# Batch 4's q turned by the DMA crossbar instead of TensorE, with new orders for every queue: linear attention and channel mix on one core

## Chip, cores and metric

The kernel runs on one core of a Trainium2 chip. The metric is the device time of one execution in microseconds. Before the change the median of three runs is 194.63 us (194.57 to 195.22).

## What is computed

For 8 batches of 8 heads, 576 positions and 64 dimensions, linear attention is followed by a gated channel mix over 512 channels:

```
q_s = softmax(q, over d);  k_s = softmax(k, over the sequence)
x   = q_s @ (k_s^T @ v)                     per head, joined to [8, 576, 512]
xk  = mu_k * x + (1 - mu_k) * x_prev        x_prev: x one position earlier
xr  = mu_r * x + (1 - mu_r) * x_prev
out = sigmoid(xr @ w_r) * (relu(xk @ w_k)^2 @ w_v)
```

w_k is 512 x 1024, w_v 1024 x 512, w_r 512 x 512. Inputs and output are float32; the products are made in bf16.

## The kernel before

The work is cut two ways. The **attention** part goes by batch b (0 to 7) and group g (0 or 1, four heads each). For each (b, g), GpSimd's queue (POOL) loads q, k and v as `load{b}{g}{q,k,v}` of 576 KB (288 KB halves for batch 1) into one of eleven `raw` buffers. ACT takes exponentials (`expq`, `expk`, L337) and casts v to bf16 (`cast`, L343). DVE sums, inverts and scales q (`rsum` L352, `rrec` L356, `scale` L361). The scaled q lies with positions on the partitions; to be multiplied with the 64 x 64 matrix of a head it has to be turned so that channels lie there. That is done in one of two ways:

- On TensorE: 36 transposes (L376) into a PSUM pair `att`, and a copy by ACT (`qt`, L384).
- Over the DMA crossbar: one DMA transpose on SP's queue, SBUF to SBUF (`qt`, L525). `CROSSBAR` lists the (b, g) that go this way: batches 5 to 7 before the change.

TensorE gathers a group's attention work in **blocks** that nothing interrupts. `TKV{b}{g}` and `B{b}{g}` make the transposes and k^T v (`kv`, L406) of a group; B makes first the x of the group before (`x`, L545). For crossed batches, `M{b}` (function `together`) makes k^T v of both groups of batch b and then the x of whatever groups are pending; M8 only x. Before the change that is TKV20, B21, TKV30, B31, B40, B41, M5 (one x), M6 and M7 (two x each), M8. `X11` and `X21` stand alone. What follows a block on DVE is `rz` and `w` (the reciprocal of k's sums and the head matrices; one operation each where the block lies in an `att` pair, two half ones where it lies in two `mm` banks), then on ACT copies of x (`xb`, `xs`), and on DVE `edge`, `diff`, `sc` and `mix` (L566 to L580), which write xk and xr into rings of four batches: `mix{b}{g}0` for xk, `mix{b}{g}1` for xr, with another digit for the halves of group 1 of batch 1.

The **channel mix** goes by units 0 to 9: 512 positions each, 256 in units 4 and 9. `k{unit}{f}` (L673) is one of eight blocks of xk @ w_k, four matmuls; `relu` (ACT, L660) and `sq` (DVE, L664) follow it. `r{unit}{m}` (L709) is 128 positions of xr @ w_r, with `th` (tanh on ACT, L714) behind it. `v{unit}{m}{h}` (L729) is a part of the second product; `o` (DVE, L735) gates it, and `st` stores it in two halves (L745), nearly all from SP's queue. The k, r and v matmuls use four PSUM banks `mm`; a bank is free again when relu, th or o has read it. The first units are cut finer: a k of units 0 and 1 comes in parts (`k11`, `k11.2`, `k11.3`), because the channels of group 1 come later.

The order on each engine and in each queue is a list written out by hand, `ORDER`: one token for each operation, with the buffer it takes behind a colon. An engine works strictly in this order and waits at each operation for what it needs; POOL and SP, which issue DMAs, do too. At most eight loads of POOL are in flight: each also waits for the landing of the one eight before it. A token `a^b` makes a wait additionally for b; none is used before the change, though the function `ordered` reads it. Fills at the start keep TensorE busy while the first loads land.

Of the kernel before, what the change touches and what calls it, by code (L numbers as in the profile page):

```python
# [55 lines left out]
expk010:1 fill.19:3 fill.20:1 fill.21:1 T01:3 kvn00:0 wp000:0 edge00 KV010:2 X000:1.0 x0001  # L56
expk011 KV011 Z01 load10v0 wk11 qt01:1 rz01:1 edge01 kvn01:1 x0000 load11q0:7 load10k0 mu:2
k02:3 cast101:0 expq100:2 k01:0 wp010:1 X010:1.0 k00:1 mucopy wp011 x0101 x0100 fill.22:2 k03:2
expq101 load11q1 wr rsum100:2 wp001 load11k1:8 rrec100 k03.2 relu03:0 sq03:0 k00.2 k02.2
relu00:1 X011:0.1 relu02:2 x0110 rsum101 expk101:2 k01.2 load11k0 cast100 sq02 scale100:2  # L60
load11v0:9 relu01:0 X001:0.3 k06:1 x0010 load11v1 wv0 expq110:0 wv1 x0111 k04:0 x0011 expk100
sq01 wv2 rrec101 scale101 TKV10:1 rsum110:3 rz10:2 w10:0 relu06:2 sq00 expq111 sq06 k05:2
relu04:0 k07:3 qt10:2 relu07:1 relu05:2 r00:1 r01:0 r03:3 rsum111 rrec110 rrec111 expk111:0
expk110 r02:2 sq05 wv3 scale111:0 cast110:1 sq07 scale110 cast111 B11:0.1 rz11:0 w11:1
load20v0:10 load20q0:0 load30q0:2 th01:0 load20k0:1 th02:1 v010:0 sq04 v000:2 th00:2 v030:1
xb10:0 v001 v031 xs10 v011 edge10 diff10:0 sc1000:0 sc1001 load21q0:3 qt11:3 th03:3 X11:1.0
xs11:1 xb111 v032 v002 load21k0:5 xb110 load21v0:4 v033 v020:3 v012 sc1010:1 mix100 edge11
cast200:2 v003 v013 v021 sc1011 diff110:1 diff111 load60k0:6 load30v0:7 v022 o03 k13:1 sc1100:2
o00 st00.2 sc1101 mix1100 mix1101 v023 load30k0:8 o01 load40k0:9 k11:2 st03.2 k11.2 k11.3
sc1110:0 expq200:1 load31q0:10 expq300:2 o02 mix101 k13.2 sc1111 relu11:2 k15:0 sq11:1 rsum200:0  # L70
k13.3 load40q0:0 k10:3 mix111 k10.2 expk200:1 k10.3 k17:2 relu15:1 k12:0 rrec200 k12.2 relu13:0
sq15 expq210:0 k12.3 r12:1 relu10:2 load31k0:2 relu17:1 expk210:2 scale200:1 k16:3 st00
load31v0:1 sq13 rsum210:1 TKV20:0 load51k0:3 sq17 rz20:1 relu12:0 cast210:0 rrec210 relu16:1
w20:2 r13:2 qt20:1 r11:0 st02.2 st02 scale210:2 k14:3 sq10 th11:4 relu14:2 sq12 th12:5 rsum300:2
B21:1.0 r20:0 xs20:0 rz21:2 xb20 load51v0:5 w21:0 qt21:0 rrec300 sq14 edge20 sq16 diff20:0 r10:3
v100:1 scale300:0 th13:6 st01.2 th20:2 X21:0.1 xs21:1 xb21 sc2010:2 v120:2 expk300:0 th10:1
sc2000:1 edge21 sc2001 diff21:1 v130:0 cast300:1 sc2100:0 expq310:1 v131 v101 load40v0:4 sc2101
mix200 expq400:0 expk310:1 o13 mix210 v110:3 v121 o10 sc2011 load70q0:8 load41v0:7 k24:0
load51q0:10 TKV30:1 rsum310:3 rrec310 relu24:0 v111 rz30:0 st13.2 k23:1 load41k0:0 cast310:2
expk400:2 sq24:0 o11 w30:1 sc2111:1 load41q0:2 k27:0 sc2110 o12 relu23:2 k20:3 k26:2 qt30:2  # L80
cast400:0 relu27:1 k21:1 scale310:1 mix211 B31:0.1 st13 sq23 relu21:0 mix201 sq27 k22:0 rz31:1
sq21 relu20:2 xb30:1 relu22:1 st03 w31:2 st11.2 st11 r23:1 xs30 rsum400:0 sq20 rrec400 sq22
th23:6 qt31:3 scale400:2 r22:3 edge30 th22:3 relu26:0 r30:0 diff30:0 sq26 sc3011:0 sc3010 k25:1
B40:1.0 v220:3 relu25:2 xb31:0 xs31 v200:2 th30:4 sc3001:1 v230:1 sq25 load61k0:1 load50q0:9
sc3000 edge31 expk410:0 v231 cast510:1 mix300 diff31:1 sc3100:2 sc3101 rz40:2 v201 cast410:2
expq410:2 load61v0:4 o23 v221 st01 w40:0 mix310 k41:0 r21:1 st12 o20 o22 st22.2 relu41:1
expq510:1 k40:2 v210:0 rsum410:1 rrec410 k42:3 load71q0:0 th21:0 sq41:1 st23 load50v0:5 relu40:0
relu42:2 k46:1 sq40 relu46:1 sc3111:1 qt40:1 st22 k37:2 expq500:0 scale410:0 st20.2 k33:3 k44:1
v211 rsum510:2 sq46 relu37:0 sq42 sc3110 expk510:1 B41:0.1 mix301 sq37:0 k34:2 relu44:1
load50k0:7 rrec510 rz41:0 o21 load60q0:2 relu33:2 mix311 w41:1 k45:1 k43:3 expk500:2 sq33 sq44  # L90
rsum500:3 relu43:0 xs40:1 relu45:2 k30:0 sq45 sq43 relu34:1 xb40 st20 k47:3 rrec500 relu47:2
scale500:1 st10 edge40 r33:1 th33:3 sq47 r31:2 diff40:0 st12.2 scale510:2 st10.2 k31:3 th31:2
relu30:0 load71k0:10 cast500:0 st23.2 r41:1 v410:2 k35:0 v411 sc4011:2 load60v0:9 expq600:2
load71v0:3 load61q0:7 relu31:2 th41:5 rsum600:0 o41 r40:3 sq31 sc4010 qt41:0 th40:1 load70k0:5
k36:1 sq30 relu35:2 mix401 sc4000:0 rrec600 qt50:2 sq34 relu36:0 M5:1.1 st41.2 k32:0 cast600:2
relu32:1 r32:1 st41 rz51:1 rz50:2 sc4001 sq35 xb41:0 w50:2 w51:0 sq32 v400:0 xs41 mix400
# [24 lines left out]
relu80:1 sq80 r82:3 st61.2 th81:5 relu82:1 th82:0 th83:1 sq82 v810:0 v800:1 v811 o81 v820:3 v821
o82 st82 st81 v801 st81.2 o80 r90:2 sq90 v830:0 v831 sq93 th90:6 st80.2 st82.2 st73.2 v900:3
v901 r91:1 o83 o90 st80 st83 st83.2 st90 st73 v910.2:2 th91:2 v911.2 o91.2 st90.2 st91.4 v910:0
v911 o91 st91.3 st91 st91.2
# [786 lines left out]
```

## Time and profile before

| what | value |
|---|---|
| median of three runs | 194.63 us |
| the profiled execution | 195.4 us |
| its span, first to last instruction | 193.6 us |
| granted TensorE clock | 0.995 |
| DMA, mean over the span | 216 GB/s, 41.86 MB |

The page gives busy times by engine, the chain of work that ended last, and the costliest groups of instructions. The chain in order of time, the timeline of an engine (start and length of each instruction, with the idle time before it and what ended that), the busy times by stretches and the DMA issues with their times to landing are views of the same trace. A row of the timeline with xN stands for N instructions merged, by start of the first; a matmul's length includes its way through the array, so the distance from start to start is what it costs.

### The profile page before, as it was taken

The numbers are of one execution on the slowest core, as the hardware profiler recorded it, in microseconds if no ns is written. First come the engines' busy times: TensorE is split into PE (matmuls) and PEld (weight loads), VectorE is DVE, ScalarE is ACT, GpSimd is POOL, SyncE is SP. The second block draws the span as 40 slices with busy tenths as digits, with TensorE's granted clock in tenths as the row PEclk, the third lists the DMA queues.
The fourth block names the chain that finished last, engine by engine and source line by source line (L and its number), as shares of the span: only waits on it lengthen the run. The fifth ranks groups of instructions, "written<-read, shape, count | busy, mean of one in ns | idle before, by whom it ended". The sixth has DMA issues, their size and how long they took to land.

```text
span 193.6 us, 4674 instructions
## 1 busy us (share of the span) xinstructions
PE 184.6 (95%) x1830; PEld 89.6 (46%) x1830; DVE 154.6 (80%) x368; ACT 138.8 (72%) x226; POOL 41.3 (21%) x65
## 2 busy tenths in 40 slices
PE   7698889999999999999999999999999999999991
PEld 2263344444545544655454544454444445554450
DVE  1788965999999999999999899997986494661521
ACT  3688899899999999899999878258425742357010
POOL 8346457453415402421200000000000000000000
PEclk9999999999999999999999999999999999999997
DMA  5999999999999997999990294253065003720085
GB/s 187 311 314 283 298 329 247 404 390 416 398 393 390 406 412 268 317 359 413 284 290 3 50 201 83 62 123 78 0 136 116 3 0 81 166 51 5 11 204 164
DMA packets 23614, 41.86 MB, mean 216 GB/s; under 512 B 9372, under 2 KB 12712, under 8 KB 23592
## 3 DMA queue, kind: packets, MB, share of 16 engines
q0 software_dynamic: 9392, 27.99, 43.3%
q1 hardware_dynamic: 13384, 12.14, 24.6%
q10 hardware_dynamic: 816, 1.44, 2.5%
q8 instruction: 14, 0.23, 0.5%
q14 instruction: 8, 0.07, 0.1%
HBM read 33.56 MB, written 9.44 MB: 222 GB/s over the span
## 4 chain that ended last, share of the span: by engine, by line
PE 84%; DMA 11%; POOL 2%; issue 0%; DVE 0%; POOLq 0%
PE mm_a L729 9%; PE mm_a L673 9%; PE mm_b L673 9%; PE mm_d L729 8%; PE mm_c L729 8%; PE mm_b L729 7%; DMA wk_ab<-in_moe_w_k_dram 6%; PE mm_c L673 6%; PE mm_b L709 6%; PE mm_d L673 5%; DMA wr<-in_moe_w_r_dram 5%; PE mm_d L709 4%; PE mm_a L709 4%; PE mm_c L709 3%; PE att_b L545 1%; PE att_a L545 1%
## 5 line engine op out<-in xcount | busy, mean ns | idle before, releaser
L729 PEld LDWEIGHTS <-k_a 128*128 128x128 bf16 x152 | 14.6, 98 | 15.6 <-issue 0.5
L729 PEld LDWEIGHTS <-k_b 128*128 128x128 bf16 x144 | 13.9, 98 | 16.4 <-issue 0.2
L709 PEld LDWEIGHTS <-xr 128*128 128x128 bf16 x144 | 13.7, 98 | 16.6 <-DMA wr<-in_moe_w_r_dram 0.6
L709 PE MATMUL mm_b<-wr,xr 128*128 128x512 bf16 x48 | 12.5, 379 | 0.1
L673 PEld LDWEIGHTS <-wk_aa 128*128 128x128 bf16 x80 | 7.5, 98 | 8.7 <-issue 1.3
L673 PEld LDWEIGHTS <-wk_bb 128*128 128x128 bf16 x80 | 7.8, 98 | 7.7 <-DMA wk_bb<-in_moe_w_k_dram 0.2
L673 PEld LDWEIGHTS <-wk_ab 128*128 128x128 bf16 x80 | 7.7, 98 | 7.7 <-DMA wk_ab<-in_moe_w_k_dram 0.2
L673 PEld LDWEIGHTS <-wk_ba 128*128 128x128 bf16 x80 | 7.5, 98 | 8.2 <-issue 1.1
L709 PE MATMUL mm_d<-wr,xr 128*128 128x512 bf16 x36 | 9.2, 379 | 0.0
L664 DVE TENSOR_TENSOR k_b<-rel_b 128x512 bf16<-128x512 bf16 (+1 forms) x15 | 5.7, 381 | 4.4 <-ACT rel_b L660 4.2
L709 PE MATMUL mm_a<-wr,xr 128*128 128x512 bf16 x32 | 8.2, 379 | 0.0
L660 ACT ACTIVATE rel_a<-mm_b 128x512 bf16<-128x512 f32 (+1 forms) x8 | 4.7, 583 | 4.4 <-PE mm_b L673 2.3
L664 DVE TENSOR_TENSOR k_a<-rel_c 128x512 bf16<-128x512 bf16 (+1 forms) x14 | 5.6, 399 | 2.4 <-ACT rel_c L660 2.3
L660 ACT ACTIVATE rel_c<-mm_b 128x512 bf16<-128x512 f32 (+1 forms) x9 | 5.3, 590 | 3.0 <-PE mm_b L673 3.0
L673 PE MATMUL mm_b<-xk,wk_ab 128*128 128x512 bf16 x24 | 7.3, 379 | 0.0
L660 ACT ACTIVATE rel_b<-mm_a 128x512 bf16<-128x512 f32 (+1 forms) x7 | 4.2, 602 | 4.2 <-PE mm_a L673 4.2
L709 PE MATMUL mm_c<-wr,xr 128*128 128x512 bf16 x28 | 7.2, 379 | 0.0
L673 PE MATMUL mm_b<-xk,wk_aa 128*128 128x512 bf16 x24 | 7.2, 380 | 0.0
L664 DVE TENSOR_TENSOR k_a<-rel_a 128x512 bf16<-128x512 bf16 (+1 forms) x16 | 6.1, 384 | 1.2 <-ACT rel_a L660 1.2
L673 PE MATMUL mm_a<-xk,wk_ba 128*128 128x512 bf16 (+1 forms) x24 | 6.9, 370 | 0.0
L673 PE MATMUL mm_a<-xk,wk_bb 128*128 128x512 bf16 (+1 forms) x24 | 6.9, 370 | 0.0
L664 DVE TENSOR_TENSOR k_b<-rel_c 128x512 bf16<-128x512 bf16 (+1 forms) x14 | 5.4, 385 | 1.7 <-ACT rel_c L660 1.3
(395 smaller groups left out, 553.1 us busy)
## 6 DMA issues: line engine op xcount, KB each, us to landing
raw_a<-in_q_dram POOLq DMA_DIRECT2D x3, 576.0 KB, 8.9
raw_c<-in_q_dram POOLq DMA_DIRECT2D x3, 576.0 KB, 9.7
raw_e<-in_v_dram POOLq DMA_DIRECT2D x3, 576.0 KB, 11.6
out_dram<-th_g SPq DMA_DIRECT2D x13, 128.0 KB, 2.4
out_dram<-th_d SPq DMA_DIRECT2D x12, 128.0 KB, 5.0
out_dram<-th_b SPq DMA_DIRECT2D x10, 128.0 KB, 4.2
out_dram<-th_a SPq DMA_DIRECT2D x10, 128.0 KB, 2.3
raw_b<-in_k_dram POOLq DMA_DIRECT2D x2, 576.0 KB, 10.9
```

The lines of the kernel that those rows point to most:

```text
L545: kn.nc.tensor.matmul(kn.half(slot, u)[two[r], to:to + n], lhsT=kn.ws[w.index][two[u], r, :], rhs=x_columns(r, u, at, n), start=True, stop ...
L660: kn.nc.scalar.activation(out=kn.rels[rel.index][:, 0:n], in_=kn.bank(kf)[:, 0:n], func=ACT.Relu, scale=HALF_ROOT)
L664: kn.nc.vector.tensor_tensor(out=kn.k2s[k2.index][:, fc, 0:n], in0=kn.rels[rel.index][:, 0:n], in1=kn.rels[rel.index][:, 0:n], op=ALU.mult)
L673: kn.nc.tensor.matmul(kn.bank(kf)[:, 0:n], lhsT=kn.wk[fc // 4][ct % 2][:, ct // 2, (fc % 4) * 128: (fc % 4) * 128 + 128], rhs=kn.xs[0][:, ...
L709: kn.nc.tensor.matmul(kn.bank(rps), lhsT=kn.xs[1][:, ct, c:c + 128], rhs=kn.wr[:, ct, :], start=(ct == 0), stop=(ct == CT - 1))
L729: kn.nc.tensor.matmul(kn.bank(vps)[:, 0:width], lhsT=kn.k2s[k2.index][:, ft, 128 * m:128 * m + 128], rhs=wv_of(ft)[:, part], start=(ft == ...
```

## The change

`CROSSBAR` begins at batch 4, so batch 4's two q are turned by DMAs on SP, and TensorE's blocks become TKV20, B21, TKV30, B31, M4 (k^T v of both groups of batch 4, and the x of group 1 of batch 3), M5, M6, M7 (two x each) and M8. Three waits are added with `^`: the turn of (4, 0) waits for the load of (6, 0)'s q, the load of (6, 1)'s q waits for the turn of (5, 1), and the turn of (6, 0) waits for the load of (7, 1)'s q. The rest of `ORDER` is new on every engine and queue. Cut to its core, with the stretches that the prediction speaks of:

```diff
-CROSSBAR = tuple((b, g) for b in range(5, B) for g in range(2))
+CROSSBAR = tuple((b, g) for b in range(4, B) for g in range(2))
 ORDER = """
...
-load20v0:10 load20q0:0 load30q0:2 ... load20k0:1 ... load21q0:3 ... load21k0:5 ... load21v0:4 ... load60k0:6
+load21q0:10 ... load20q0:0 ... load20v0:2 load21k0:1 ... load30q0:3 ... load20k0:4 ... load51k0:6 ... load21v0:7
...
-k16:3 ... TKV20:0 ... cast210:0 rrec210 relu16:1 ... r13:2 qt20:1 r11:0 ... k14:3 ... B21:1.0 r20:0
+expk200:2 r10:3 k14:1 relu17:0 st02 cast210:0 TKV20:1 rz20:1 relu15:2 rrec210 relu14:1 r13:0 ... r20:2 r11:1 ... B21:0.1
...
-B40:1.0 ... qt40:1 ... B41:0.1 ... qt41:0 ... qt50:2 ... M5:1.1 ... qt51:3 ... M6:1.0.1 ... qt60:1 ... qt61:0
+M4:0.0 ... qt40^load60q0:0 ... qt41:1 qt50:2 ... st22 ... st22.2 ... qt51:3 ... M5:1.1.0 ... load61q0^qt51:10
+... M6:0.1.0 ... load70v0:3 load71k0:8 load70k0:4 ... load71q0:6 ... qt60^load71q0:0 qt61:1
...
-r91:1 o83 o90 st80 st83 st83.2 st90 st73 v910.2:2 th91:2 v911.2 o91.2 st90.2 st91.4 v910:0 v911 o91 st91.3 st91 st91.2
+r91:2 o81 v910.2:3 st83.2 st81 th91:4 v911.2 o91.2 st90.2 st81.2 v910:1 st91.4 st91.3 v911 o91 st91 st91.2
 """
```

More of the change, by code (lines that the diff above doesn't have):

```diff
@@ L49 @@
 ACT!load00q0:0 zero ident load00q1 ACT!load00k0:1 load01q1:2 ACT!load01q0 rows load00v consts
-warm load00k1 load01v late load01k0:3 load10v1:4 wk00 load10q0:5 expq001:0 expq000 load10q1
-rsum001:0 ACT!load01k1 rsum000 wk01 expq011:1 rrec001 load10k1:6 rrec000 rsum011:1 fill:1
+warm load00k1 load01v late load01k0:3 load10q0:4 wk00 load10q1 expq001:0 expq000 load11q0:5
+rsum001:0 ACT!load01k1 rsum000 wk01 expq011:1 rrec001 load10k0:6 rrec000 rsum011:1 fill:1
 fill.2:2 fill.3:3 fill.4:0 fill.5:1 fill.6:2 fill.7:3 fill.8:0 fill.9:1 fill.10:2 fill.11:3
@@ L55 @@
 fill.26:3 fill.27:1 KV001:0 rrec011 scale010:1 KV000 T00:1 rest Z00 qt00:0 scale011 rz00:0
[L56 to L96, printed above, removed]
@@ L121 @@
[L121 to L124, printed above, removed]
+expk010:1 fill.19:3 fill.20:1 fill.21:1 T01:3 kvn00:0 wp000:0 edge00 wp001 wk11 mu:0 fill.22:1
+load10k1 X000:1.0 mucopy expk011 KV010:2 KV011 Z01 qt01:1 x0001 expq100:2 edge01 rz01:1 kvn01:1
@@ new lines @@
+x0000 X001:0.3 x0010 load10v0:7 load10v1 load11q1 expq101 k03:0 wr wp010:1 X010:1.0 k02:1 x0011
+expq110:0 x0100 wp011 x0101 rsum100:2 k00:2 k01:3 k02.2 rrec100 rsum101 relu02:0 sq02:0 k03.2
+k01.2 rrec101 relu03:1 expk100:2 X011:0.1 scale100:2 x0110 relu01:2 k00.2 rsum110:3 expk101
+relu00:0 k05:1 load11v0:8 k04:0 cast100:0 cast101 rrec110 scale101 k06:3 x0111 k07:2 expq111
+load11k0:9 sq01 sq03 sq00 scale110:0 relu06:2 TKV10:0 r03:3 relu05:1 relu07:0 load11k1 rz10:2
+r02:1 sq06 relu04:2 load11v1 w10:0 rsum111 sq05 wv0 qt10:2 cast110:1 expk110:0 sq07 sq04 expk111
@@ new lines @@
+rrec111 r01:2 wv1 r00:0 wv2 cast111 scale111 th03:0 wv3 th02:1 th00:2 B11:1.0 xs10:0 xb10
+load21q0:10 v020:3 rz11:0 w11:1 edge10 v010:1 load20q0:0 v000:0 v001 qt11:3 diff10:0 v021 v011
+load20v0:2 load21k0:1 v022 X11:0.1 sc1000:0 v023 sc1001 sc1010:1 xs11:1 v012 load30q0:3 xb110
+sc1011 mix100 v013 edge11 xb111 th01:3 expq210:1 v002 load20k0:4 expq200:2 o02 load51k0:6
+diff111:1 load21v0:7 diff110 o01 load31q0:5 k13:3 sc1100:2 v003 sc1101 v030:2 o00 load31v0:9
+mix1100 mix1101 k11:1 sc1110:0 v031 v032 v033 k11.2 k11.3 load40q0:8 o03 k10:0 cast200:2
@@ new lines @@
+rsum200:0 sc1111 relu11:1 load40v0:10 st00 expk210:1 rrec200 k13.2 sq11:1 k13.3 k10.2 mix111
+k10.3 relu10:0 k16:2 relu16:2 sq16 k12:1 k12.2 load40k0:0 mix101 sq10 expq300:0 relu13:1 k17:0
+k12.3 load30v0:2 st00.2 load30k0:1 scale200:1 k15:2 load41v0:3 rsum210:1 relu12:2 sq12 sq13
+expk200:2 r10:3 k14:1 relu17:0 st02 cast210:0 TKV20:1 rz20:1 relu15:2 rrec210 relu14:1 r13:0
+w20:2 st01.2 load50v0:4 load31k0:7 st02.2 r20:2 r11:1 scale210:2 qt20:0 th13:4 th20:5 rsum300:2
+B21:0.1 rrec300 sq14 th11:6 rz21:2 th10:2 sq15 w21:0 xb20:1 v110:0 r12:2 scale300:0 v130:1 xs20
@@ new lines @@
+sq17 edge20 v131 qt21:1 X21:1.0 diff20:0 th12:1 sc2001:2 expq400:2 xs21:0 xb21 load50k0:8 sc2000
+v111 o13 mix200 st01 expq310:1 cast400:1 edge21 diff21:1 load41q0:5 v100:3 cast300:2 sc2100:0
+cast310:0 sc2101 load51q0:10 load41k0:2 mix210 sc2011:1 expk300:0 o11 v101 v120:2 v121 o12
+rsum310:3 k25:1 sc2111:2 k24:0 st13 rrec310 k21:2 o10 load61v0:9 relu24:1 sc2010 TKV30:0
+relu21:2 sc2110 st10 st10.2 st11.2 k20:0 st12 sq24:0 k22:3 mix211 k23:2 relu25:0 rz30:0 w30:1
+sq21 k26:1 expk400:2 expk310:1 relu22:1 k27:3 mix201 sq25 relu20:2 sq22 qt30:2 relu27:0
@@ new lines @@
+scale310:1 sq20 r21:0 rsum400:0 sq27 relu26:1 load70q0:1 relu23:2 sq23 r23:3 cast410:2 B31:1.0
+rrec400 th23:3 v230:1 rz31:1 sq26 xs30:0 st03 st03.2 v231 xb30 v200:2 v201 scale400:2 w31:2
+edge30 expk410:0 r30:3 th21:2 diff30:0 qt31:3 load51v0:0 load60v0:7 st12.2 sc3010:0 o23 M4:0.0
+load50q0:3 o20 sc3001:2 r22:2 load60k0:2 expq410:0 th30:0 load71v0:5 xs31:1 xb31 th22:1
+cast510:0 sc3000 st11 cast500:1 v220:3 v221 mix300 rz40:2 rz41:0 w40:0 w41:1 load61k0:0 st20.2
+v210:0 edge31 diff31:1 sc3101:1 expq510:1 sc3100 load60q0:4 v211 mix310 sc3110:2 k47:1 relu47:0
@@ new lines @@
+k44:2 o22 k40:3 sc3111 relu44:2 o21 k45:1 sq44:1 k41:2 rsum410:1 sq47 st13.2 rrec410 k42:0
+relu40:1 st21 sc3011 expq500:2 k30:3 relu45:2 k31:1 sq40 mix311 st21.2 sq45 relu42:0 sq42
+relu30:1 sq30:0 k34:0 relu31:2 mix301 sq31 k43:3 relu43:0 relu41:1 rsum500:2 k35:1 k46:3 r41:2
+relu35:2 th41:6 sq43 rrec500 r31:1 sq41 relu46:0 k33:2 th31:4 k32:3 scale410:0 relu34:1 st20
+r33:1 expk500:1 k37:0 sq46 scale500:1 qt40^load60q0:0 relu32:0 rsum510:3 v410:3 v411 sq34
+expq600:0 qt41:1 qt50:2 sq35 st22 relu37:1 k36:0 rrec510 th33:2 r40:1 scale510:2 sq37 o41 st22.2
@@ new lines @@
+rsum600:0 expk510:0 qt51:3 relu33:2 M5:1.1.0 sq32 load61q0^qt51:10 cast610:2 sq33 rz50:1 w50:2
+rz51:2 relu36:1 th40:5 xb40:1 sq36 rrec600 xs40 edge40 diff40:1 xs41:0 w51:0 sc4001:1 v300:0
+v400:1 v401 xb41 expq700:2 cast600:0 v301 sc4011:2 o40 edge41 v310:2 expk610:2 o30 st40.2 sc4000
+diff41:0 v311 r32:3 sc4101:0 mix400 v330:1 sc4100 v320:0 sc4010 th32:1 sc4110:1 sc4111 mix410
+expk600:0 v321 st40 v331 o32 o31 expq610:1 k55:3 k50:0 o33 st41.2 st30.2 relu55:0 relu50:2 k57:2
+relu57:1 M6:0.1.0 k52:3 mix411 sq55:1 mix401 xb51:0 load70v0:3 load71k0:8 load70k0:4 rsum610:1
@@ new lines @@
+st31.2 rz61:0 rz60:1 w61:1 relu52:0 k53:2 k51:3 w60:0 st31 xs51 st41 xs50:1 r51:0 scale600:0
+sq52 sq50 r52:1 xb50 relu51:0 relu53:2 st33.2 edge50 diff50:1 edge51 sq51 th51:5 diff51:0 st32
+sq57 cast710:1 sc5001:0 sc5101:1 sq53 r53:3 k54:2 th53:4 th52:6 st33 expk710:1 k56:0 rrec610
+sc5000 sc5010:2 r50:3 sc5100 mix510 relu54:0 mix500 v520:1 load71q0:6 relu56:1 v500:2 sc5011
+sq54 sc5111:1 k64:0 sq56 v501 scale610:1 expq710:0 th50:2 k61:3 mix501 o50 relu64:2 cast700:0
+relu61:0 rsum710:2 k65:0 relu65:1 expk700:0 rrec710 qt60^load71q0:0 qt61:1 st50 v521 v530:2 v531
@@ new lines @@
+k75:1 o61 o60 k73:0 k74:3 relu75:0 relu73:2 th63:0 qt70:3 sq73 relu74:2 sq76 M8:0.1.0 k70:2
+v620:3 xb70:1 st61 xs70 edge70 diff70:1 sc7010:1 mix611 v621 o62 sc7000:2 relu70:1 st61.2 v630:2
+xs71:0 v631 sc7001 o63 xb71 sq70 edge71 k77:0 relu77:1 st63 st62.2 r80:1 r72:3 r73:2 th80:5
+th73:4 r71:0 v700:1 st63.2 sq75 sq74 diff71:0 st62 sc7100:0 th71:0 th72:2 sc7101 mix710 mix700
+k94:2 sc7011 relu94:0 k96:0 k95:3 k92:2 sq77 v701 relu96:2 v730:0 sq96:0 o70 relu92:1 sq92
+v710:2 v731 v711 o73 st73.2 k90:1 relu95:2 v720:3 v721 sc7111:0 st70.2 st60 k86:0 mix701 o71
@@ new lines @@
+k91:2 sq94 sc7110 o72 mix711 k84:3 relu91:1 sq95 sq91 st23 st72 st71.2 relu90:0 st60.2 relu86:2
+k97:2 relu97:1 sq97 relu84:1 k80:1 sq86:1 sq90 relu80:2 sq84 k81:0 relu81:0 k82:2 relu82:1 sq82
+k93:3 relu93:1 sq93 sq80 r81:1 k87:0 k85:2 relu85:1 relu87:2 sq81 sq85 k83:3 relu83:0 st71
+st72.2 st23.2 sq87 r82:2 th81:1 sq83 v820:0 st73 v800:3 r83:1 v821 th83:0 th82:2 v801 v830:1 o80
+st80.2 st70 o82 r90:2 v900:3 v901 th90:3 o90 st82 st90 st80 v831 st82.2 o83 st83 v810:0 v811
+r91:2 o81 v910.2:3 st83.2 st81 th91:4 v911.2 o91.2 st90.2 st81.2 v910:1 st91.4 st91.3 v911 o91
@@ L125 @@
+st91 st91.2
 """
```

30 lines of the change are left out of this document (6 added, 24 removed).

## The prediction

> **What bounds the kernel now.** I read the page first: the span, the busy times, the chain that ended last.
>
> ```profile
> span 193.6 us, 4674 instructions
> PE 184.6 (95%) x1830; PEld 89.6 (46%) x1830; DVE 154.6 (80%) x368; ACT 138.8 (72%) x226; POOL 41.3 (21%) x65
> PE 84%; DMA 11%; POOL 2%; issue 0%; DVE 0%; POOLq 0%
> ```
>
> The chain is TensorE for 84% and DMA for 11%. The chain in order of time tells where the change-over is:
>
> ```profile
> 18.00 9.29 DMA wr<-in_moe_w_r_dram
> 27.33 1.04 PE mm_b L709 x4
> ...
> 189.61 0.42 DVE th_c L735
> ```
>
> Until 27.33 us the load of `wr` decides; from there TensorE runs without a visible gap to 189.57, then one gate, one store and its landing fill the rest of the 193.6. The table by stretches shows how little room the others have early on:
>
> ```profile
> 40.00:55.00 15.00, 14.97 (x200) 6.95 (x198) 14.97 (x30) 14.61 (x23) 5.78 (x8) 1.00 1.04 401
> ```
>
> The columns are PE, weight loads, DVE, ACT, POOL, granted clock (1.00), DMA share, GB/s. Between 40 and 55 us PE, DVE and ACT are all full and the DMA engines move 401 GB/s. So work taken from TensorE after 27.33 is worth its full time, and an operand that comes late there costs its full lateness: nothing makes it good afterwards.
>
> **The change, part by part.**
>
> *Batch 4 leaves TensorE's transposes.* Blocks B40 and B41 (the x of the group before, 36 transposes, 36 kv products each) go; M4 (both kv, one x) comes, and M5 takes two x in place of one. A block is measured here from where the next plain matmul would have started, which is 0.43 us after the start of a row with x2 (0.22 for x1), to the start of the first plain one behind it.
>
> ```profile
> 71.70 0.38 PE L673 MATMUL mm_b<-xk,wk_bb 128*128 128x512 bf16 x1
> ...
> 73.00 0.60 PE L729 MATMUL mm_d<-wv_a,k_a 128*128 128x512 bf16 x2
> ...
> 84.25 0.59 PE L729 MATMUL mm_a<-wv_d,k_a 128*128 128x512 bf16 x2
> ...
> 85.77 0.60 PE L673 MATMUL mm_c<-xk,wk_ba 128*128 128x512 bf16 x2
> ...
> 96.15 0.59 PE L673 MATMUL mm_b<-xk,wk_bb 128*128 128x512 bf16 x2
> 97.77 0.61 PE L673 MATMUL mm_a<-xk,wk_aa 128*128 128x512 bf16 x2
> ```
>
> ```profile
> 109.44 0.59 PE L729 MATMUL mm_b<-wv_d,k_a 128*128 128x512 bf16 x2
> 111.26 0.61 PE L673 MATMUL mm_a<-xk,wk_ba 128*128 128x512 bf16 x2
> ```
>
> ```profile
> 128.17 0.59 PE L729 MATMUL mm_b<-wv_d,k_b 128*128 128x512 bf16 x2
> 129.90 0.61 PE L673 MATMUL mm_b<-xk,wk_aa 128*128 128x512 bf16 x2
> ```
>
> B40: 73.00 - 71.92 = 1.08. B41: 85.77 - 84.68 = 1.09. M5, with one x: 97.77 - 96.58 = 1.19. M6 and M7, with two x: 1.39 and 1.30. Now 1.08 + 1.09 + 1.19 = 3.36; afterwards 1.19 + 1.35 = 2.54. The change takes **0.82 us** from TensorE (0.78 to 0.87).
>
> *What goes with it on the other engines.* ACT loses two copies of q, and DVE does batch 4's weights in halves:
>
> ```profile
> 82.14 1.11 ACT L384 COPY qt_b<-att_b 128x1152 bf16<-128x1152 bf16 x1
> ```
>
> ```profile
> 77.37 0.28 DVE L423 TENSOR_TENSOR w_a<-att_b,rz_c 128x128 bf16<-128x128 f32 x1
> 99.04 0.28 DVE L428 TENSOR_SCALAR w_c<-mm_c,rz_c 128x64 bf16<-128x64 f32 x1
> ```
>
> ACT gains about 2 us; DVE pays two more operations of 0.28 and two small reciprocals, under 0.8 us. Neither is on the chain, so nothing for both; if DVE were late the 0.8 us would count, and it stands in the upper end.
>
> *The front.* Before `wr`, POOL's queue has in both orders the same batch 0 v, eight loads of 288 KB and four of `wk`; only which one stands where differs. So `wr` should land at 27.3 again. The new order does all of unit 0's k before batch 1's first block, and that block waits for v, which moves to two places ahead of `wr`; it still ends before 27.3. Cost: nothing, from -0.2 to +0.3. The tail has the same last five PE operations and the same two last stores on SP: nothing, up to 0.3 if SP's queue backs up.
>
> *The new order of loads, 40 to 52 us.* Here I find a wait. In the new order POOL loads batch 5's k (load51k0) ahead of load21v0, which becomes the eighth load from load21q0 on instead of the seventh from load20v0. On ACT, `cast210` waits for it; behind `cast210` stand relu15, relu14 and qt20; relu15 frees the PSUM bank that r20 takes on PE. First when PE is ready for r20, by pitches:
>
> ```profile
> 30.89 0.22 PE L545 MATMUL att_a<-qt_c,w_a 64*64 64x64 bf16 x4
> ...
> 32.04 0.61 PE L729 MATMUL mm_a<-wv_a,k_a 128*128 128x512 bf16 x2
> ...
> 34.21 0.59 PE L729 MATMUL mm_a<-wv_b,k_a 128*128 128x512 bf16 x2
> ...
> 35.10 0.60 PE L729 MATMUL mm_b<-wv_c,k_a 128*128 128x512 bf16 x2
> ```
>
> ```profile
> 60.01 0.59 PE L673 MATMUL mm_a<-xk,wk_bb 128*128 128x512 bf16 x2
> ...
> 61.32 0.60 PE L729 MATMUL mm_d<-wv_c,k_b 128*128 128x512 bf16 x2
> ```
>
> ```profile
> 51.32 1.04 PE L709 MATMUL mm_a<-wr,xr 128*128 128x512 bf16 x4
> ```
>
> B11 is 1.15 (30.89 to 32.04), X11 0.46 (35.10 - 34.64), a block like TKV20 0.87 (61.32 - 60.44, rounded down), a matmul 0.216. In the new order 72 matmuls stand between B11 and r20: 30.89 + 1.15 + 0.46 + 0.87 + 72 x 0.216 = 48.9. In the old one 76 and B21 (1.08) did, which makes 50.87; the row says 51.32. So the kernel before lost **0.45 us** here to small waits of its own; their operations stand elsewhere in the new order, and I let them go.
>
> Now when ACT is ready. Loads land one after the other; with no stores beside them they come 1.51 us apart, as two that ACT waited for show:
>
> ```profile
> 38.21 1.16 ACT L337 ACTIVATE eq_b<-raw_a 128x1152 bf16<-128x1152 f32 x1 [0.35 <-DMA raw_a<-in_q_dram]
> 39.73 1.16 ACT L337 ACTIVATE eq_c<-raw_c 128x1152 bf16<-128x1152 f32 x1 [0.35 <-DMA raw_c<-in_q_dram]
> ...
> 47.53 1.14 ACT L343 CAST vv_a<-raw_e 128x1152 bf16<-128x1152 f32 x1
> 48.63 0.60 ACT L660 ACTIVATE rel_b<-mm_d 128x512 bf16<-128x512 f32 x1
> ```
>
> The eighth load in the trace of before, its issue on POOL and its time to landing:
>
> ```profile
> 35.76 0.72 POOL L211 DMA_DIRECT2D raw_g<-in_k_dram  x1 [0.61 <-ACT xb_b L557]
> ```
>
> ```profile
> raw_g<-in_k_dram POOLq DMA_DIRECT2D x1, 576.0 KB, 12.6
> ```
>
> It landed at 35.76 + 12.6 = 48.4, though six loads after 38.2 would make 47.2 without stores: the unit 0 stores, issued from 39.09 to 43.45, took the rest.
>
> ```profile
> 39.09 0.54 SPq L745 DMA_DIRECT2D out_dram<-th_c  x1
> ...
> 42.85 0.59 SPq L745 DMA_DIRECT2D out_dram<-th_a  x1
> ```
>
> The new order has as many stores there, starting some 0.9 us later behind a later gate, so load21v0 lands between 47.2 and 48.4; I take 48.1, near the row with stores. Then cast210 from 48.15, relu15 1.10 later (47.53 to 48.63), 0.60 long: the bank is free at 49.85. PE stands from 48.9: **0.93 us** (0.2 to 1.2). Inside it lies a smaller wait ahead: k11's second part needs mix1100, which gets one more gate in front of it on DVE.
>
> ```profile
> 37.51 0.67 DVE L735 SCALAR_TENSOR_TENSOR th_d<-th_d,mm_b 128x512 f32<-128x512 f32 x1
> 38.11 0.35 DVE L575 TENSOR_SCALAR xm_c<-xd_b,mu 128x576 bf16<-128x576 bf16 x1
> ...
> 39.27 0.81 DVE L580 TENSOR_TENSOR xk<-xm_c,xb_b 128x576 bf16<-128x576 bf16 x2
> ```
>
> One gate is 0.60 (37.51 to 38.11), so both halves end near 40.7, where PE wants the second at 40.5: about 0.2, swallowed by r20's wait or left alone if that one goes.
>
> *Turns kept apart.* On SP the turn of 40 waits for load60q0, and 41, 50, two stores and 51 queue behind it; on POOL load61q0 and four loads queue behind the turn of 51. M5 is the first to want 40 and 41. In the trace its plain start is 96.58; the new order has k32 and M4 ahead of it in place of B40 and B41 (0.86 + 1.19 - 2.17 = -0.1) and the wait above (0.93 - 0.45), which makes 97.0. A turn lands 3.2 us after issue:
>
> ```profile
> qt_c<-qs_c SPq DMA_TRANSPOSE x1, 3.2
> ```
>
> ```profile
> 81.60 1.35 DVE L361 TENSOR_TENSOR qs_a<-eq_c,rrec_b 128x1152 bf16<-128x1152 bf16 x1
> ```
>
> The scaled q of 41 ended at 82.95; the new order puts fifteen more DVE operations ahead of it (one reduction like the 1.35 of this row, the others of the 0.3 to 0.8 kind of the rows above), an estimated 6 us, and perhaps 2 us of waits: 89 to 91, landed by 94.2. The 2.8 us left hide the turn, so nothing is charged.
>
> **Sum**: -0.82 - 0.45 + 0.93 = -0.34. The profiled execution's own 195.4 becomes 195.1, its span 193.6 becomes 193.3; the median of the runs, 0.8 below that execution, 194.63, becomes **194.3**.
>
> **Rivals.** (1) *The load is in time.* load21v0 lands at 47.2 and r20 stands for no more than the 0.25 of k11: -0.82 - 0.45 + 0.25 = -1.0, **193.6**. For it: the 1.51 us pitch of loads; against it: 48.4 in the trace with stores in flight. (2) *The turns come late*, and the kernel is slower. Place: M5. Each us by which the turn of 41 is issued after 93.8 costs one us of PE, since M5 heads PE's queue. It takes 2.8 us more delay on DVE, or turns that run one behind the other at more than 3.2 us: with two queued turns of 5 us, landed at 91 + 8 = 99, M5 waits 2.0: 194.3 + 2.0 = **196.3**. For it: the one turn with a landing was alone; against it: 2.8 us of room. [...] (3) *The old waits do not go, and new ones of their kind come*: the 0.45 stays and as much again is lost where DVE and ACT are full: 194.3 + 0.9 = **195.2**. (4) *Nothing gained*: blocks cost what they did; 0.82 more, **195.1**; the block rows speak against it.
>
> **How the numbers follow.** Forecast 0.45 (193.9 to 194.7 by the load's landing); rival 1 0.23, 2 0.12, 3 0.15, 4 0.05. A measurement of this kernel tells about 0.5% from no change: 193.66 and 195.60. Below: most of rival 1, 0.17. Above: rival 2 and a third of rivals 3 and 4, with a little for the DVE charge, 0.22. Between: 0.61. The range leaves out the best tenth and the rest of rival 2: 193.4 to 196.0.
>
> **What would show it.** B40 and B41 gone, M4 about 1.2 us long, M5 about 1.35. `wr` landing at 27.3 and r03 starting then. ACT idle before cast210 with a DMA named, and PE idle ahead of r20 with ACT named, near 49 us, 0.5 to 1 us. No PE idle before M5. The prediction is wrong if PE shows other gaps after 27.33 that add to over half a us, or if the chain holds a crossbar turn.

## The result, and the profile after

The changed kernel takes 195.72 us in the median of 17 runs (194.88 to 196.61), the kernel before 194.87 us beside it (194.38 to 195.28). The ratio is 1.0047, with an interval of 1.0035 to 1.0059: slower by a half per cent, where 194.3 was forecast, slightly faster.

The profiled execution of the changed kernel (194.88) is the fastest of its 17, and that of the kernel before (195.40) is slower than any of the 17 beside it. So a second profile of each, from one chip, stands beside them below. First the page of the changed kernel, with span, busy times and the chain that ended last:

```profile
span 193.1 us, 4559 instructions
PE 183.9 (95%) x1758; PEld 89.1 (46%) x1758; DVE 153.7 (80%) x372; ACT 137.4 (71%) x226; POOL 41.3 (21%) x65
...
PE 76%; DMA 11%; DVE 6%; POOL 2%; ACT 1%; issue 1%; POOLq 0%; ACTq 0%
```

TensorE lost 0.7 us of busy time and ACT 1.4, as the crossbar took its work. The chain holds DVE for 6% now. Its way in order of time, from the load of `wr` on:

```profile
17.79 8.55 DMA wr<-in_moe_w_r_dram
26.39 1.04 PE mm_d L709 x4
...
40.46 1.26 DVE rsum_a L352
44.45 1.27 DVE qs_b L361
45.72 1.26 DVE rsum_b L352
49.04 1.02 PE mm_c L709 x4
...
187.20 0.89 PE mm_b L729 x8
```

`wr` decides the start as before, and the chain leaves TensorE ahead of 49.04, where r20 begins. From 36 to 48 us it runs along DVE. It gets there from `relu15` by a semaphore row of ACT's sequencer at 48.09 that belongs to `qt20`, and passes by the cast that ran on ACT until 48.49. So the 6% of DVE are not what r20 waited for; the rows below and the experiment on the load tell that. The stretch that had no room before, in the busy times from 40 to 55 us:

```profile
40.00:55.00 15.00, 14.24 (x192) 6.84 (x190) 14.12 (x27) 13.97 (x23) 5.17 (x8) 1.00 1.04 401
```

PE is busy for 14.24 us of 15 where it was 14.97. The 0.73 us that are missing can be one hole or several. TensorE's timeline, and then ACT's, show one:

```profile
47.24 1.04 PE L709 MATMUL mm_a<-wr,xr 128*128 128x512 bf16 x4
49.04 1.02 PE L709 MATMUL mm_c<-wr,xr 128*128 128x512 bf16 x4 [0.76 <-ACT rel_c L660]
```

```profile
47.34 1.15 ACT L343 CAST vv_a<-raw_h 128x1152 bf16<-128x1152 f32 x1 [0.86 <-DMA raw_h<-in_v_dram]
48.40 0.59 ACT L660 ACTIVATE rel_c<-mm_c 128x512 bf16<-128x512 f32 x1
```

This is the wait that the prediction placed: `cast210` waits for load21v0, relu15 comes behind it, and r20 on PE behind relu15. From start to start r13 to r20 takes 1.79 (before rounding) where four matmuls take 0.86: 0.93 us. The blocks, on TensorE's timeline:

```profile
74.16 1.03 PE L709 MATMUL mm_d<-wr,xr 128*128 128x512 bf16 x4
...
76.08 1.04 PE L709 MATMUL mm_c<-wr,xr 128*128 128x512 bf16 x4
...
95.12 1.03 PE L709 MATMUL mm_b<-wr,xr 128*128 128x512 bf16 x4
...
97.29 0.60 PE L729 MATMUL mm_a<-wv_a,k_a 128*128 128x512 bf16 x2
```

Measured as in the prediction, M4 takes 76.08 - 75.02 = 1.06 and M5 97.29 - 95.98 = 1.31. No PE idle stands ahead of M5: the turns are in time. Now the end, on SP's queue and on DVE:

```profile
184.84 0.59 SPq L745 DMA_DIRECT2D out_dram<-th_c  x1
185.54 2.38 SPq L745 DMA_DIRECT2D out_dram<-th_a  x2
188.01 1.19 SPq L745 DMA_DIRECT2D out_dram<-th_b  x2
189.30 1.33 SPq L745 DMA_DIRECT2D out_dram<-th_e  x2
```

```profile
188.11 0.42 DVE L735 SCALAR_TENSOR_TENSOR th_e<-th_e,mm_b 128x256 f32<-128x256 f32 x1 [0.40 <-PE mm_b L729]
```

The last gate ends at 188.53, and the last two stores are issued from 189.30 to 190.63. In the kernel before, the gate of 189.61 ended at 190.03, and the second of the last two stores followed it by 0.18 us:

```profile
189.56 1.19 SPq L745 DMA_DIRECT2D out_dram<-th_c  x2
```

After the change SP is over a us behind: two stores at 185.54 took 2.38 us to issue, where two take 1.2 elsewhere. Where the time went, from the four profiles:

| us | before | before, second | after | after, second |
|---|---|---|---|---|
| own time | 195.40 | 194.58 | 194.88 | 195.14 |
| first r starts | 27.33 | 26.77 | 26.39 | 26.98 |
| from there to the end of the last matmul | 162.24 | 161.99 | 161.69 | 161.89 |
| from there to the end of the span | 4.0 | 4.1 | 5.0 | 4.4 |

The start differs by chance more than by kernel. The middle is a little shorter than before. The end is longer by 0.3 to 1.0 us, where nothing had been expected, or 0.3 at most.

### The profile page after: what moved, and what is told of

Its sections match the earlier page's. It is cut to its first block, busy times and chain, and to the rows that moved or that the text cites. A ratio compares the mean times of both kernels' runs of the same rounds, so it can differ in the third digit from the quotient of the medians.

```text
span 193.1 us, 4559 instructions
## 1 busy us (share of the span) xinstructions
PE 183.9 (95%) x1758; PEld 89.1 (46%) x1758; DVE 153.7 (80%) x372; ACT 137.4 (71%) x226; POOL 41.3 (21%) x65
## 4 chain that ended last, share of the span: by engine, by line
PE 76%; DMA 11%; DVE 6%; POOL 2%; ACT 1%; issue 1%; POOLq 0%; ACTq 0%
PE mm_d L729 9%; PE mm_a L729 8%; PE mm_d L673 7%; PE mm_b L729 7%; PE mm_a L673 7%; DMA wk_ab<-in_moe_w_k_dram 6%; PE mm_c L729 6%; PE mm_c L673 6%; PE mm_c L709 6%; PE mm_b L673 5%; PE mm_b L709 4%; DMA wr<-in_moe_w_r_dram 4%; PE mm_d L709 3%; PE mm_a L709 2%; PE att_a L545 1%; PE att_b L545 1%
## 5 line engine op out<-in xcount | busy, mean ns | idle before, releaser
L709 PE MATMUL mm_c<-wr,xr 128*128 128x512 bf16 x48 | 12.3, 379 | 0.8 <-ACT rel_c L660 0.8
L660 ACT ACTIVATE rel_b<-mm_c 128x512 bf16<-128x512 f32 (+1 forms) x9 | 4.6, 507 | 9.8 <-PE mm_c L673 9.4
L709 PE MATMUL mm_b<-wr,xr 128*128 128x512 bf16 x40 | 10.3, 379 | 0.0
L660 ACT ACTIVATE rel_a<-mm_d 128x512 bf16<-128x512 f32 (+1 forms) x10 | 5.6, 555 | 4.0 <-PE mm_d L673 3.8
L673 PE MATMUL mm_a<-xk,wk_bb 128*128 128x512 bf16 (+1 forms) x28 | 8.1, 371 | 0.0
L673 PE MATMUL mm_a<-xk,wk_ba 128*128 128x512 bf16 (+1 forms) x28 | 8.1, 371 | 0.0
L673 PE MATMUL mm_d<-xk,wk_aa 128*128 128x512 bf16 (+1 forms) x28 | 7.7, 356 | 0.0
L673 PE MATMUL mm_d<-xk,wk_ab 128*128 128x512 bf16 (+1 forms) x28 | 7.7, 356 | 0.0
L664 DVE TENSOR_TENSOR k_a<-rel_b 128x512 bf16<-128x512 bf16 (+1 forms) x15 | 5.7, 381 | 1.9 <-ACT rel_b L660 1.7
L553 ACT CAST xb_a<-att_a 128x1024 bf16<-128x1024 f32 x5 | 5.3, 1052 | 2.0 <-DVE xr L580 1.4
```

Source lines behind the costliest of these rows:

```text
L553: kn.nc.scalar.copy(out=kn.xbs[xb.index][:, h, 64:576], in_=kn.whole(pair)[:, h, :])
L660: kn.nc.scalar.activation(out=kn.rels[rel.index][:, 0:n], in_=kn.bank(kf)[:, 0:n], func=ACT.Relu, scale=HALF_ROOT)
L664: kn.nc.vector.tensor_tensor(out=kn.k2s[k2.index][:, fc, 0:n], in0=kn.rels[rel.index][:, 0:n], in1=kn.rels[rel.index][:, 0:n], op=ALU.mult)
L673: kn.nc.tensor.matmul(kn.bank(kf)[:, 0:n], lhsT=kn.wk[fc // 4][ct % 2][:, ct // 2, (fc % 4) * 128: (fc % 4) * 128 + 128], rhs=kn.xs[0][:, ...
L709: kn.nc.tensor.matmul(kn.bank(rps), lhsT=kn.xs[1][:, ct, c:c + 128], rhs=kn.wr[:, ct, :], start=(ct == 0), stop=(ct == CT - 1))
```

## The experiments

The theory at first: the load behind r20 and a backed-up SP queue cost what the blocks give. All are edits of the changed kernel unless it says before. Each was timed beside runs of the kernel before on the same chip.

**The kernels as they are.**

> The changed kernel as it is. Theory A (front): its first profile had wr landing at 26.3 us, 0.9 us earlier than the kernel before, and was the fastest of 17 runs; a typical execution has wr at about 27.2, and that is the 0.85 us by which the median (195.72) stands above that profile (194.88). Theory B (tail): the spread is in the last stores, which SP issues late; then wr lands near 26.3 again and the time from the end of the last matmul to the end of the span moves between 4 and 6 us. Ratio to before by either: 1.003 to 1.006.

> The kernel before as it is, for a second profile: its first (195.4) was slower than its median (194.87) by 0.5. If it is typical this time: about 194.8, wr landing at 27.3 or a little ahead, small waits of PE of 0.3 to 0.8 us after 27 us, 4.05 us from the end of the last matmul to the end of the span.

Measured: the changed kernel 195.32 (194.93 to 195.79), ratio 1.0026 (1.0011 to 1.0040); before 194.58, a typical run. Both theories of the spread are half right: `wr` landed at 26.93 and the first r came 0.6 us later than in the first profile, and the end shrank from 5.0 to 4.4. The wait for r20 grew, on TensorE's timeline of the second profile:

```profile
47.72 1.04 PE L709 MATMUL mm_a<-wr,xr 128*128 128x512 bf16 x3
49.84 1.02 PE L709 MATMUL mm_c<-wr,xr 128*128 128x512 bf16 x4 [1.08 <-ACT rel_c L660]
```

The idle time is 0.32 more than in the first profile, so r20 stands 1.25 us.

**The load behind r20.**

```diff
-load51k0:6 diff111:1 load21v0:7
+diff111:1 load21v0:7 load51k0:6
```

> The changed kernel with load51k0 behind load21v0 on POOL. Theory (the load sets r20's wait): load21v0 lands 1.5 us earlier, near 45.8, PE's 0.93 us ahead of r20 near 49 us goes to 0.1 or less, and the time falls by 0.5 to 0.9 us: about 194.8 to 195.2, ratio to before 0.999 to 1.002. Rival (the next late thing takes its place, as DVE and ACT are full between 40 and 55 us): the wait moves to B21 or a k a few us later, the time falls by under 0.3: 195.4 or more.

Measured: 194.08 (193.34 to 195.06), ratio 0.9959 (0.9941 to 0.9977), 1.24 less than the changed kernel on the same chip, more than expected, since the wait is 1.25 in a typical run and not 0.93. On PE and ACT of this run:

```profile
47.49 1.04 PE L709 MATMUL mm_a<-wr,xr 128*128 128x512 bf16 x3
48.37 1.03 PE L709 MATMUL mm_c<-wr,xr 128*128 128x512 bf16 x4
```

```profile
46.59 1.17 ACT L343 CAST vv_a<-raw_h 128x1152 bf16<-128x1152 f32 x1
47.64 0.63 ACT L660 ACTIVATE rel_c<-mm_c 128x512 bf16<-128x512 f32 x1
```

The cast no longer waits, r20 follows r13 after 0.88, and no other wait takes its place. The middle takes 160.66 us, 1.33 less than the second profile of before.

**Stores issued earlier.**

```diff
-st23 st72 st71.2 ... st60.2 ... st23.2 ... st73 ... st70
+st23 st60.2 st23.2 st70 st73 st72 st71.2
```

> The changed kernel with st60.2, st23.2, st70 and st73 ahead of st72 on SP, so that they are issued at 170 to 173 us, where SP stood waiting, and not between 180 and 185. Theory (SP's queue backs up at the end): four issues of 0.6 us leave the tail, the last store is issued within 0.2 us of its gate, the time from the last matmul to the end of the span falls from 5.0 to about 4.0, and the time falls by 0.7 to 1.1 us: about 194.7 to 195.0. Rival (the end is set by the landing of the last stores, whatever their issue): no change, 195.5 to 195.9.

Measured: 195.45 (194.56 to 196.20), ratio 1.0025 (1.0005 to 1.0045): no change, and still 5.0 us at the end. SP again spent 1.66 us on one store, and the last store was issued 1.5 us behind its gate. The edit did less than was meant: from 180 us on SP issues twelve stores in the changed kernel and eleven here, and the nine from 184 us on are the same, since three of the four moved stores had been issued before 171 us anyhow. So this run decides neither theory. It shows that the stall lies in the issue of a single store, and something slows that issue itself. The table of DMA queues of the second profile of the changed kernel, from 185 to 188 us, shows what else was there (queue, kind, packets, MB, share of 16 engines):

```profile
q1 hardware_dynamic: 255, 0.43, 59.5%
q8 instruction: 1, 0.02, 1.9%
```

One packet of kind "instruction", 16 KB, held a DMA engine for 1.9% of 16 x 3 us = 0.9 us. Such packets come through the whole run, by the packets' records some 6 to 25 us apart. In the kernel before, the last one of this queue lies between 173 and 175 us, with no store under way:

```profile
q8 instruction: 1, 0.02, 4.4%
```

The change takes 144 rows out of TensorE's instruction stream (3660 to 3516 by the two pages, weight loads included). With two rows for each matmul of 0.216 us, TensorE goes through 9.3 per us. That this queue brings TensorE's instructions, in step with its rows, was the author's estimate here; if it does, fewer rows let the same fetch come later. A store can meet it: in the kernel before, one that runs alone keeps DMA engines busy, from 125.1 to 125.5 us, for 101.7% of the time of 16 (a packet counts whole where it starts), so it uses all of them, also one that a fetch holds. That became the new theory to be tested: the cost of a fetch depends on where it falls.

**The fetch moved, first try.** The fills at the start are cut in four, which adds rows and no work.

```diff
-matmul(bank[:, 0:512], ...)
+for a in range(n): matmul(bank[:, 0:512 // n], ...)      # n = 4 for the first 14 fills (22 in the kernel before), else 1
```

> The changed kernel with 14 of the 27 fills at the start (matmuls on zeros that only keep TensorE busy; 512 columns each) cut in four of 128 columns. The same work, but 84 rows more in TensorE's instruction stream. Theory (a fetch of TensorE's instructions, a 16 KB packet of queue 8 of 0.9 to 1.5 us, falls into the last stores at 184 to 186 us and holds up one of the 16 DMA engines that every store uses): TensorE reads 9.3 rows per us, so the last fetch comes 9 us sooner, near 176, where no store is under way; the slow issue on SP (1.5 to 2.4 us for one or two stores) goes, the last store is issued within 0.2 us of its gate, and the time from the last matmul to the end falls from 4.3 to 5.1 to about 4.05. The time falls by 0.3 to 1.0: 194.5 to 195.2, ratio to before 0.998 to 1.002. Rival (the tail is long because of the order of the stores, and the fetch only happens to be there): no change, 195.3 to 195.8.

> The kernel before with 22 of its fills cut in four: 132 rows more in TensorE's stream. Its last fetch was at 174 us, between two groups of stores; 14 us sooner it comes at 160, and one more fetch comes near 182 to 185, into the last stores (from 182 us on). Theory (the fetch): a slow issue on SP appears, 4.05 us from the last matmul to the end become 4.4 to 5.1, and the time rises by 0.3 to 1.0: 195.1 to 195.8, ratio 1.002 to 1.005. Rival (the order of the stores): no change, ratio 0.999 to 1.001.

> The changed kernel with load51k0 behind load21v0 and 14 fills cut in four: both repairs. If the load and the fetch are the two things that cost, the gains add: 194.08 less 0.3 to 1.0, that is 193.1 to 193.8, ratio to before 0.991 to 0.995. If the fetch is nothing: 194.1, ratio 0.996.

Measured: 195.89 (ratio 1.0043, 1.0021 to 1.0065), 198.81 (1.0201, 1.0176 to 1.0226) and 194.55 (1.0005, 0.9972 to 1.0038). The end did what the theory says: 4.0 us in the first and the third, 5.2 in the kernel before. The totals did not, because the edit is not neutral. With cut fills the granted clock falls at the start in two of the three runs, in the changed kernel to 0.50 from 18 to 20 us; the busy times of the kernel before with cut fills show it in the column after the engines (PEclk):

```profile
18.00:20.00 2.00, 2.00 (x22) 0.93 (x23) 1.58 (x6) 1.22 (x2) 1.28 (x2) 0.57 1.17 283
20.00:22.00 2.00, 2.00 (x9) 0.82 (x8) 0.88 (x4) 0.05 (x1) 1.07 (x2) 0.57 1.07 400
```

In these 4 us the granted clock is 0.57, and the first r starts at 29.89, though `wr` landed at 26.69. Ahead of the fall TensorE stood for 2.21 us amid matmuls of one kind, for nothing that the profile shows ("issue"), and a packet of q8 had begun at 13.79:

```profile
16.12 0.21 PE L406 MATMUL mm_a<-vb_b,ek_b 64*64 64x64 bf16 x1 [2.21 <-issue]
```

The other two runs with cut fills stand there too (1.47 and 1.48 us), and no profile with whole fills has such a stand; in the third run the clock did not fall (1.00 from 16 to 44 us). That TensorE had run out of instructions there is not shown, and neither is that the stand brought the clock down.

The third run shows a stalled store in the middle as well. Beside a fetch at 153.3 us one of three stores took SP 1.78 us:

```profile
152.77 0.59 SPq L745 DMA_DIRECT2D out_dram<-th_c  x1
153.41 1.78 SPq L745 DMA_DIRECT2D out_dram<-th_a  x1
155.24 0.60 SPq L745 DMA_DIRECT2D out_dram<-th_c  x1
```

```profile
157.74 0.38 PE L673 MATMUL mm_a<-xk,wk_ba 128*128 128x256 bf16 x2 [0.75 <-ACT th_a L714]
```

ACT's tanh into `th_a` has to wait until those stores have read it, first in the kernel with the load and the rows repaired (below), where the fetch comes at 151.7 and slows none of these stores, then here:

```profile
155.67 0.60 ACT L714 ACTIVATE th_a<-mm_a 128x512 f32<-128x512 f32 x1 [0.46 <-DMA out_dram<-th_a]
```

```profile
157.09 0.60 ACT L714 ACTIVATE th_a<-mm_a 128x512 f32<-128x512 f32 x1 [1.63 <-PE mm_c L673]
```

The matmul named in the second row is not what it waited for: the r in its own bank had ended by 155.7. The slow store landed 3.7 us after its issue, at 157.1, and there the tanh starts. ACT idles 1.63 us in place of 0.46, and PE, which needs the bank that this tanh reads, 0.75. So these three tell the end apart, and not the total. A cleaner edit was needed.

**The fetch moved, without touching the start.** Unit 5's k and r matmuls (in the kernel before, the r of unit 6 too) are cut in two halves of 256 columns.

```diff
-for ct in cts: matmul(bank[:, 0:n], ..., rhs=xs[:, ct, c0:c0 + n])
+for a in (0, 256): for ct in cts: matmul(bank[:, a:a + 256], ..., rhs=xs[:, ct, c0 + a:c0 + a + 256])
```

> The changed kernel with unit 5's k and r matmuls (48, 512 columns wide) each cut in two of 256 columns: the same columns in the same time, 96 rows more in TensorE's stream, from about 115 us on; the fills at the start are as they were. Theory (the fetch of TensorE's instructions in the last stores): the last fetch comes 10 us sooner, near 175, with no store under way; from the last matmul to the end 4.0 us in place of 4.3 to 5.1, and the time falls by 0.3 to 1.0: 194.4 to 195.2. Rival (the order of the stores): 195.3 to 195.8, as it was. If cutting a matmul costs more than its rows, TensorE's part grows by at most 48 x 0.02 = 1 us.

> The kernel before with the k of unit 5 and the r of units 5 and 6 (64 matmuls) cut in two, the start as it was: 128 rows more. Theory (the fetch): the fetch at 174 us comes near 160, the next one near 184, into the last stores; from the last matmul to the end 4.4 to 5.2 us in place of 4.04, and the time rises by 0.3 to 1.1: 195.1 to 196.0, ratio 1.002 to 1.006. Rival: ratio 0.999 to 1.001.

> The changed kernel with load51k0 behind load21v0, and unit 5's k and r cut in two. If both the load and the fetch cost what they seem to: 194.1 less 0.3 to 1.0, so 193.1 to 193.8, ratio to before 0.991 to 0.995, with 4.0 us from the last matmul to the end. If the fetch is nothing: 194.1, ratio 0.996.

Measured, with the kernel before at 194.78: the changed kernel with 96 rows more takes 194.62 (194.38 to 194.86), ratio 0.9986 (0.9977 to 0.9995). The kernel before with 128 rows more takes 196.20 (195.75 to 197.09), ratio 1.0073 (1.0054 to 1.0092). Both repairs together take 193.23 (193.00 to 193.59), ratio 0.9919 (0.9906 to 0.9932). The theory holds from both sides, and in the kernel before the fetch costs more than expected (1.4 us). SP's queue at the end, first of the changed kernel with more rows, then of the kernel before with more rows:

```profile
185.67 0.59 SPq L745 DMA_DIRECT2D out_dram<-th_c  x1
186.36 1.19 SPq L745 DMA_DIRECT2D out_dram<-th_a  x2
187.65 1.19 SPq L745 DMA_DIRECT2D out_dram<-th_b  x2
188.93 1.18 SPq L745 DMA_DIRECT2D out_dram<-th_e  x2
```

```profile
183.66 0.54 SPq L745 DMA_DIRECT2D out_dram<-th_d  x1
184.25 2.09 SPq L745 DMA_DIRECT2D out_dram<-th_a  x1
186.38 0.60 SPq L745 DMA_DIRECT2D out_dram<-th_e  x1
```

In the one the stall of 2.38 is gone, with the same stores in the same order, and the end is 4.0 us. So it was not the order or the number of the stores. In the other, one store now takes 2.09, and the end is 5.3. The same store in the second profile of before:

```profile
184.21 0.59 SPq L745 DMA_DIRECT2D out_dram<-th_a  x1
```

The queue table has the packet between 177 and 179 us in the one:

```profile
q8 instruction: 1, 0.02, 4.4%
```

and between 184 and 187 us in the other:

```profile
q8 instruction: 1, 0.02, 3.5%
```

The last matmul ends at 188.90 in the one (188.87 in the changed kernel) and at 188.79 in the other (188.76 in the kernel before): cutting costs TensorE nothing, and all of the difference lies behind it.

All 14 profiles together agree. In the eight in which a packet of q8 falls among the last stores, the end takes 4.4 to 5.7 us; in the other six it takes 4.0 to 4.1. Of the 1106 stores that SP issued in the 14, 27 took 0.9 us or more, and each of these overlaps such a packet. Another 37 overlap one and took 0.47 to 0.85 us, so a fetch beside a store does not always stall it.

**The added waits.**

```diff
-qt40^load60q0:0 ... load61q0^qt51:10 ... qt60^load71q0:0
+qt40:0 ... load61q0:10 ... qt60:0
```

> The changed kernel without its three added waits between turns and loads; order and buffers as they are. Theory (TensorE waits for no turn, and the held loads are not late): no change, 195.3 to 195.8, ratio to before 1.002 to 1.005. Rival A (the waits hold loads or stores up and cost something): faster by over 0.4. Rival B (turns and loads do disturb each other): turns land over 5 us after issue, TensorE waits at M5 or M6, slower by over 0.5.

Measured: 195.61 (195.06 to 196.72), ratio 1.0040 (1.0023 to 1.0058), between the two results of the changed kernel. TensorE waits for no turn here either, though the turn of (4, 0) now landed 7.9 us after its issue, where it took 3.3 in the second profile of the changed kernel. So rival B had the late turn right and the wait at M5 wrong. The three waits cost nothing that this can show, and no gain in time shows either.

**`wr` one load earlier,** on top of the repaired load.

```diff
-load10v1 load11q1 ... wr
+load10v1 wr load11q1
```

> The changed kernel with load51k0 behind load21v0, and the load of wr one place earlier on POOL, ahead of the last half of (1, 1)'s q. In the changed kernel TensorE stands 0.8 to 2.0 us in one piece ahead of the first r for wr; in the kernel before it stands there for little. Theory (wr decides the front): wr lands 0.7 to 0.9 us earlier, near 25.9, the first r starts there, and the time falls by 0.5 to 0.9: 193.2 to 193.6, ratio 0.991 to 0.994. Rival (q of (1, 1), now later, holds block B11 near 30 us and takes the gain back): 194.0 or more.

Measured: 197.13 (196.30 to 197.91), ratio 1.0115 (1.0094 to 1.0136), 3 us worse than without. `wr` landed at 26.12, but the first r came later. ACT's timeline, PE's, and the busy times:

```profile
26.93 0.68 ACT L337 ACTIVATE eq_a<-raw_f 128x576 bf16<-128x576 f32 x1 [2.37 <-DMA raw_f<-in_q_dram]
27.52 0.58 ACT L660 ACTIVATE rel_c<-mm_d 128x512 bf16<-128x512 f32 x1
```

```profile
28.15 1.07 PE L709 MATMUL mm_d<-wr,xr 128*128 128x512 bf16 x3 [2.66 <-ACT rel_c L660]
```

```profile
28.00:32.00 4.00, 3.85 (x11) 1.41 (x11) 3.17 (x8) 4.00 (x8) 3.36 (x5) 0.57 1.23 212
```

The late q holds ACT's exponential; the relu behind it frees the bank that the first r takes. That is the shape of r20's wait again, 20 us earlier. TensorE stood 2.66 us and was then granted 0.57 of its clock for 4 us. The rival had the mechanism, at another place than B11, and missed the clock. Against the profile with the load alone repaired, the first r comes 1.4 us later, the middle takes 1.7 longer, and the end 0.6, where a fetch again met a store (2.13 us).

## Why the prediction was wrong

**The blocks: right, a little small.** Forecast -0.82; M4 and M5 take 1.06 + 1.31 = 2.37 in place of 3.36, which is -0.99.

**The old waits: gone, as forecast, but the first profile had more of them than the second.** Forecast -0.45. From B11 to r20 the kernel before takes 20.43 us in its first profile and 20.14 in its second, where the pitches make 19.98: waits of 0.45 and 0.16. With the load repaired it is 18.06, where the pitches of the new order make 18.03, so nothing of them is left. The prediction had read one execution that is slower than any of the 17.

**The new wait at r20: place and mechanism right, its typical size above the 0.93 forecast.** It was 0.93 in the first profile and 1.25 in the second. Moving its load gave 1.24 of the median. The forecast range went to 1.2. That the first profile hits 0.93 is in part luck: the load landed at 47.3 and not at 48.1, and TensorE was ready at 48.1 and not at 48.9, both 0.8 us early, as `wr` had landed early.

**Start and turns: right.** The first r came at 26.39 and 26.98, before at 27.33 and 26.77, so no cost within what single executions vary. The turns were in time (41's was issued at 89.87, forecast 89 to 91). DVE's four operations more did not count (busy 154.6 us before, 153.7 after). Rivals 2 and 4 didn't happen. (The 91 + 8 in rival 2 is not two turns of 5 us, which would make 101; nothing hangs on it.) Of rival 1 the landing came true (47.3 for its 47.2), but r20 stood all the same. Rival 3 comes near the measured time, and not by its mechanism: besides r20's wait, no gap of TensorE over 0.2 us shows after the first r in either profile. So the signs of being wrong that the prediction named stayed away; none of them looked behind the last matmul.

**The tail: this is the step that failed.** "The tail has the same last five PE operations and the same two last stores on SP: nothing, up to 0.3 if SP's queue backs up." The operations were the same, and the time wasn't: 0.3 to 1.0 us more in the two profiles. With the fetch out of the last stores the median falls from 195.32 to 194.62 (ratios 1.0026 and 0.9986 to the kernel before). The reason allowed for was another one too: SP did fall behind, but where a fetch of TensorE's instructions fell among its stores, and the fetch came there (its packet begins at 185.5 us in the first profile, the last one before the change at 174.3) because the change shortened TensorE's stream by 144 rows: 96 rows more brought it back to 177.5. The forecast counted the time of the removed instructions and not their number.

The sum of the middle by the second profiles: -0.99 - 0.16 + 1.25 = +0.1, where -0.34 was forecast and -0.1 measured (161.89 against 161.99); the 0.2 between them is not accounted for. The tail adds 0.7 by the experiment: +0.6 to +0.8, and 0.5 to 0.85 was measured. With the fetch moved, the change is faster by 0.16 us in place of the 0.34 forecast. By the three terms of the middle it would be slower by 0.1, so single profiles tell it to about 0.3. That the fetch stalls SP by holding one of the DMA engines that a store uses is argued, from the packet's 0.9 to 1.7 us and the lone store that kept all 16 busy; shown is that the stall comes and goes with it. Why the changed kernel's median differed by 0.4 on two occasions stays open. The kernel with the fetch moved varies by 0.5 us in 11 runs, against 0.9 and 1.7 for the changed kernel, which fits a spread by the fetch; but those runs were on another chip, so this is not shown.

## What to carry to other kernels

Count instructions as well as their time: here 96 rows more in TensorE's stream moved its last instruction fetch by 8.0 us (185.5 to 177.5), and one that fell into the last stores cost up to 1.4 us. When a load is moved ahead of another on one queue, look at what stands behind its consumer on that engine: it was a relu that freed a PSUM bank, at r20 (1.25 us) and again at the first r (2.66 us), that cost TensorE the time. To move a fetch for a test, cut wide matmuls in the middle of the run, not the fills at the start.
